# Double key loading, longer value runs and a re-planned layer norm in a fused attention and feed-forward block

## The chip, the cores and the metric

The kernel runs on one core of a Trainium2 chip. The metric is the device time of one execution in microseconds (us). A core has five engines with an instruction queue each: PE (TensorE, matrix products), DVE (VectorE), ACT (ScalarE), POOL (GpSimd) and SP (SyncE, which here issues nearly all DMAs). Each runs its own queue in order and waits on semaphores for the others. PE writes into PSUM, which has eight banks of 128 x 512 fp32; everything else lives in SBUF (128 partitions) or in device memory.

## The reference, cut to what matters

One transformer block with modulation by a condition vector c. S = 2048 positions, D = 576, H = 32 heads of 18, F = 4608, all fp32:

```python
sa, ca, ga, sb, cb, gb = six rows of (silu(c) @ w_mod)      # each of length D
h = layernorm(x) * (1 + ca) + sa
q, k, v = split(h @ wqkv)                                    # 32 heads of 18
p = softmax(q k^T * 18**-0.5)                                # 32 x 2048 x 2048
x = x + ga * ((p v) @ wo)
h = layernorm(x) * (1 + cb) + sb
out = x + gb * (silu(h @ w1) @ w2)
```

## The kernel before

**Arithmetic.** PE multiplies fp32 values in a rounded form; where that is too coarse, each operand is split into a high and a low part and three products (high-high, high-low, low-high) are added. A weight or activation therefore exists twice (`hh`/`hl`, `th`/`tl`, planes 0 and 1 of `w1t`, `w2t`, `wo`).

**Stages.** `start_tasks` (L1064) does the first layer norm, part of the q, k and v projections and the first 40 slots of scores. q and k go to device memory (`qscr`, `kscr`) in a layout that has the high and low parts of a head's 18 rows as 54 rows, v to `vscr`. Then comes attention over four blocks of 512 queries; in a block, eight quads of four heads. The output of block b is projected by `wo`, added to x, normalised again and sent through the feed-forward part while the attention of block b+1 runs. During the first block there is no feed-forward work yet, and the rest of the q and k projections fills PE instead. After the attention of the last block the feed-forward part of that block runs alone (the tail).

**Slots.** A quad of 512 queries x 2048 keys is 32 slots of two half slots. A half slot of pass a (`slot_a`, L682) multiplies 128 queries by 512 keys into a bank `psa` (`slot_mm`, L672), and DVE takes the row maximum (L680); that gives the score that softmax subtracts. 40 slots later (`LEAD`), pass b (`slot_b`, L711) computes the same scores transposed, 128 keys by 512 queries, with the maximum as two more rows of the operand, into a bank `psb`, and ACT takes the exponential into a tile `pt` (L727). The matmuls of the two passes use 64 of PE's rows each, and one of each runs at the same time. When the exponentials of a key tile (128 keys, four heads) are done, `run_pv` (L747) multiplies them by v: four heads beside each other, 32 columns of PE each, into `psv` (L762). A "value run" is the row of key tiles that are multiplied without anything between.

**Keys.** `load_k` (L645) loads 512 keys of a quad as four DMAs of 54 rows into two of 14 tiles `kts`, a ring. The same tile serves pass a and, 40 slots later, pass b. `slot_load` (L665) asks for the next keys eight slots ahead. SP issues the DMA when the tile's last reader is done.

**Order on PE.** The order of PE's instructions is written by hand, by a planner that runs while the program is built (`Plan`, L92). It keeps a time for PE and queues for ACT and DVE with fixed costs (`TS`, `TV`, `TX`, `TMAX`, `TEXP`, L73), knows when a bank comes free (`ring`, `take`, `when`), and in the main loop (L1440) chooses the next piece: a half slot, a value run of n ready key tiles, or a piece of the "filler" (q and k projections, later projection and feed-forward, L266), whose `need` says when a piece may start. `pace` spreads the filler over the slots. A value run is chosen when three key tiles are ready, when the filler has nothing ready and two are, or when there is nothing else. The other engines' instructions, the DMAs on SP among them, are ordered by the framework's own scheduler.

**Filler of a block** (`post`, L847). First `o_T` (L855) splits the attention output `ou` into `th` and `tl`; the two last row tiles wait for the time `o["at", b]` that `out_b` (L771) estimates from the last quad's DVE work. Then, for each of four row tiles, `proj` (28 pairs of half matmuls into two banks `psF`), `add_x1` and the layer norm: `ln_a` (statistics, `ln_rstd`) straight after the row tile, `ln_c` (apply) in the middle of the next. None of the layer norm's DVE work is entered in the planner's DVE queue, and `ln_at` is the plan's time plus 4500 ns. What is left of the feed-forward part of the block before (`left`) stands between the row tiles. Then the transposes `h_T`, and `mlp1`/`mlp2`. `out_b` sends the 18 rows of each head from `ov` to their place in `ou`, by SP; for the fifth row tile, of 64 rows, the rows are sent twice, to partitions 0 to 63 and 64 to 127.

**Banks.** From the first block's end on (`open_mlp`, L801) three banks are the filler's (`psF`), two row scores' (`psA`), two transposed scores' (`psB`), one the values'.

Of the kernel before, what the change touches and what calls it, by code (L numbers as in the profile page):

```python
# [18 lines left out]
P = 128  # L19
S = 2048  # L20
# [9 lines left out]
NKC = S // 512  # L30
# [13 lines left out]
NKB = 14  # L44
# [17 lines left out]
PB = 7  # L62
# [18 lines left out]
STAND = 0  # L81

# [250 lines left out]
def tile_adaln_block(ctx: ExitStack, tc: tile.TileContext, x, wqkv, wo, w1, w2, c, wfirst, wcol, out):  # L333
# [14 lines left out]
    kts = [at1.tile([P, 512], F32R, name=f"kt{i}") for i in range(NKB)]  # L348
# [26 lines left out]
    def ln_rstd(pool, mv, n):  # L375

        eng = nc.vector if pool is mp.get("p") else nc.gpsimd
        ve = pool.tile([P, n], F32, name="ve", bufs=4)
        eng.tensor_scalar_add(ve, mv[:, :, 1], EPS)
        r0 = pool.tile([P, n], F32, name="r0", bufs=4)  # L380
        nc.gpsimd.tensor_tensor(r0, ve, mhalf[:, :n], op=ALU.pow)

        t1 = pool.tile([P, n], F32, name="t1", bufs=4)
        eng.tensor_mul(t1, r0, r0)
        eng.tensor_mul(t1, t1, ve)
        eng.tensor_scalar(t1, t1, -0.5, 1.5, op0=ALU.mult, op1=ALU.add)
        rs = pool.tile([P, n], F32, name="rs", bufs=4)
        eng.tensor_mul(rs, r0, t1)
        return rs
# [196 lines left out]
    state = {"now": 0, "p": 0, "k": 0, "b": 0, "tail": False, "tail2": False}  # L586
# [42 lines left out]
    def load_quad(i):  # L629
# [13 lines left out]
        t["mx"] = at1.tile([P, 4, NST, NKC], F32, tag="mx", name="mx", bufs=2)  # L643

    def load_k(i, kc):  # L645
        qd = i % NQUAD
        for hp in range(2):
            kt_ = kts[state["k"] % NKB]
            state["k"] += 1
# [4 lines left out]
            quads.setdefault(i, {})["k", kc, hp] = kt_  # L654
# [10 lines left out]
    def slot_load(s):  # L665
# [3 lines left out]
        if (s + KLD) % 8 == 0 and 32 <= s + KLD < 32 * NQ:  # L669
            load_k(*divmod((s + KLD) // 8, 4))  # L670

    def slot_mm(s, j):  # L672
# [6 lines left out]
           rhs=t["k", kc, hp][64 * j:64 * j + 54, :], start=True, stop=True)  # L679
# [31 lines left out]
    def slot_b(s, j):  # L711
# [3 lines left out]
        if j == 0:  # L715
            if w == 0:
                t["P"] = {}
# [7 lines left out]
        mm(ps, lhsT=t["k", kt // 4, hp][64 * e:64 * e + 56, kt % 4 * P:(kt % 4 + 1) * P],  # L725
# [45 lines left out]
    def out_b(i, ov):  # L771
# [13 lines left out]
        nc.vector.transpose(ov, tt)  # L785
        chain([("V", 700), ("V", 260), ("V", 460), ("V", 700)], plan.t + 700, None, lambda at: o.update({("at", b): at + 5500}))
        for h in range(4):
            c0 = 72 * qd + DH * h
            while c0 < 72 * qd + DH * h + DH:
                kt, r0 = divmod(c0, P)  # L790
                n = min(72 * qd + DH * h + DH - c0, P - r0)
                p0 = 32 * h + c0 - 72 * qd - DH * h
                for r in (r0, r0 + 64) if kt == 4 else (r0,):
                    nc.sync.dma_start(ou[r:r + n, kt, :], ov[p0:p0 + n, :])
                c0 += n
# [5 lines left out]
    def open_mlp():  # L801
# [5 lines left out]
        psF = ctx.enter_context(tc.tile_pool(name="psF2", bufs=3, space=PSUM))  # L807
        psA = ctx.enter_context(tc.tile_pool(name="psA2", bufs=2, space=PSUM))
        mp["p"] = ctx.enter_context(tc.tile_pool(name="mlp", bufs=1, side="right"))
        plan.ring("f", 3)  # L810
        plan.ring("b", 2)
        plan.ring("a", 2)
# [34 lines left out]
    def post(b):  # L847
# [7 lines left out]
        def o_T(kt):  # L855
# [4 lines left out]
            plan.op("A", plan.t, 600)  # L860
            nc.scalar.activation(hi, src, AF.Copy)
            eng = nc.vector if last and kt % 2 == 0 else nc.gpsimd
            if kt < 4:
                eng.tensor_tensor(c["tl"][:, kt, :], src, f(hi), op=ALU.subtract)
            else:
                eng.tensor_tensor(hi[64:], src[64:], f(hi)[64:], op=ALU.subtract)
# [24 lines left out]
        def ln_a(j):  # L891
            mv = pool.tile([P, 1, 2], F32, name="mv2", bufs=4)
            ln_stats(pool, c["x1"][j], mv[:, 0, :])
            c["ln_at", j] = plan.t + 4500
            c["ln", j] = mv, ln_rstd(pool, mv, 1)

        def ln_c(j):
            mv, rs = c["ln", j]
            if j == 0:
                c["ob"] = att.tile([P, NST, 640], F32, tag="o", name="ob", bufs=1)  # L900
            ln_apply(c["x1"][j], c["ob"][:, j, :], mv[:, 0, :], rs, nc.vector)
# [655 lines left out]
```

## Time and profile before

| | |
|---|---|
| median of 3 runs | 2501.65 us (2499.65 to 2503.61) |
| profiled execution | 2500.9 us, its span 2499.1 us |
| mean granted TensorE clock | 0.984 |
| busy share of the span: PE, DVE, ACT, POOL | 96%, 72%, 60%, 25% |
| DMA | 377.78 MB, mean 151 GB/s |
| DMAs of keys (L652) | 512 of 108 KB |

How to read it: busy times are the time in which an engine had an instruction of that group under way; two matmuls at the same time count once. PEclk is the share of the full TensorE clock that was granted. A row of the view of waits has who waited, for whom, the total in us, how often, and the longest. A row of the timeline has the start in us, the length in us, the engine and line, output and inputs, how many instructions were merged, and the idle time before them with what ended it. A row of the table by stretches has, for each engine, busy us and the number of instructions, then the granted clock, the DMA share and GB/s.

### The profile page before, as it was taken

Reading aid. Unit: us, or ns where it says so; the run is one execution under the profiler, and the core shown is the slowest. Engines: PE = TensorE matmul, PEld = TensorE weight load, DVE = VectorE, ACT = ScalarE, POOL = GpSimd, SP = SyncE. Lnnn points to the kernel's source line nnn. Section 1 sums busy time; section 2 is a strip of 40 time slices with the busy share of each in tenths; the row PEclk is TensorE's granted clock in tenths of the full one; section 3 lists DMA queues with packets and bytes.
Section 4 is the critical chain, followed back from the end, with each engine's and each line's share of the span. In section 5 each row is a group of like instructions: output and inputs, shape, how many; then the busy total and the mean of one; then the engine's idle time right before and its main releaser. Section 6 shows DMA issues by size and latency. Waiting matters only on the chain.

```text
span 2499.1 us, 51105 instructions
## 1 busy us (share of the span) xinstructions
PE 2392.5 (96%) x19952; PEld 1568.9 (63%) x19952; DVE 1802.2 (72%) x3107; ACT 1495.2 (60%) x2736; POOL 633.4 (25%) x766
## 2 busy tenths in 40 slices
PE   6999999997899999998999999999999999999999
PEld 4874444434466666665666666666666666678988
DVE  7868888876788787786877777777877777324333
ACT  4237777774567666665666666665766666742121
POOL 4201111122576666653211111112211111110000
PEclk9999999998899999999999999998999999999999
DMA  7843344342465555543534333442533443226463
GB/s 241 257 137 112 113 124 124 104 149 87 134 204 178 182 188 188 179 164 127 193 129 151 128 124 129 144 141 82 204 129 130 151 146 136 96 94 236 171 224 118
DMA packets 170183, 377.78 MB, mean 151 GB/s; under 512 B 27006, under 2 KB 63262, under 8 KB 169942
## 3 DMA queue, kind: packets, MB, share of 16 engines
q1 hardware_dynamic: 165350, 372.22, 44.1%
q8 instruction: 158, 2.59, 0.4%
q10 hardware_dynamic: 4592, 2.29, 0.4%
q14 instruction: 83, 0.68, 0.1%
HBM read 282.87 MB, written 86.33 MB: 148 GB/s over the span
## 4 chain that ended last, share of the span: by engine, by line
PE 80%; DVE 9%; issue 4%; ACT 3%; DMA 2%; POOL 1%; SPq 1%; ACTq 0%; DVEq 0%; POOLq 0%
PE ps L470 25%; PE psv L762 17%; PE psa L678 13%; PE ps L464 9%; PE psb L725 8%; DVE mx L680 3%; PE psqk L551 3%; PE psv L470 2%; PE psp L470 1%; DVE etmp L988 1%; ACT pt L727 1%; DMA qt<-qscr 1%; ACT etmp L987 1%; PE psv L1213 1%; DVE hh L399 1%
## 5 line engine op out<-in xcount | busy, mean ns | idle before, releaser
L680 DVE TENSOR_REDUCE mx<-psa 128x1 f32<-128x512 f32 x2048 | 1343.7, 685 | 378.8 <-PE psb L725 269.3
L727 ACT ACTIVATE pt<-psb 128x512 f32<-128x512 f32 x2048 | 1160.0, 598 | 566.6 <-PE psb L725 413.9
L678 PE MATMUL psa<-kt,qt 54*128 54x512 f32 x2048 | 775.5, 429 | 43.6 <-DVE mx L680 39.7
L725 PE MATMUL psb<-qt,kt 56*128 56x512 f32 x2048 | 795.3, 433 | 4.4 <-ACT pt L727 2.8
L678 PEld LDWEIGHTS psa<-kt,qt 54*128 54x128 f32 x2048 | 345.3, 186 | 454.8 <-DVE mx L680 311.5
L762 PE MATMUL psv<-pt,vt 128*32 128x512 f32 x4096 | 540.9, 608 | 1.0 <-ACT pt L727 1.0
L470 PE MATMUL ps<-w2t,g 64*128 64x288 f32 x4992 | 418.6, 295 | 3.6 <-DVE x L885 3.6
L470 PEld LDWEIGHTS ps<-w2t,g 64*128 64x128 f32 x4992 | 391.3, 188 | 38.9 <-issue 10.1
L470 PE MATMUL ps<-hh,w1t 64*128 64x512 f32 x2160 | 386.6, 394 | 0.2
L725 PEld LDWEIGHTS psb<-qt,kt 56*128 56x128 f32 x2048 | 348.8, 186 | 36.1 <-ACT pt L727 24.4
L470 PEld LDWEIGHTS ps<-hh,w1t 64*128 64x128 f32 x2160 | 222.7, 186 | 54.6 <-issue 13.0
L991 POOL TENSOR_TENSOR g<-etmp,g 128x512 fp32r<-128x512 f32 x108 | 140.2, 1313 | 408.8 <-ACT g L990 408.7
L889 POOL TENSOR_TENSOR x<-x,gt 128x288 f32<-128x288 f32 x116 | 92.7, 800 | 456.2 <-ACT gt L888 456.2
L762 PEld LDWEIGHTS psv<-pt,vt 128*32 128x32 f32 x4096 | 91.2, 109 | 175.7 <-issue 165.0
L470 PE MATMUL ps<-hl,w1t 64*128 64x512 f32 x864 | 188.2, 393 | 0.0
L885 DVE TENSOR_TENSOR x<-ps,x 128x288 f32<-128x288 f32 x184 | 83.5, 454 | 119.8 <-PE ps L464 74.8
L464 PE MATMUL ps<-w2t,g 128*128 128x288 f32 x960 | 133.2, 299 | 5.1 <-ACT g L990 3.8
L464 PEld LDWEIGHTS ps<-w2t,g 128*128 128x128 f32 x960 | 130.8, 191 | 8.0 <-ACT g L990 4.3
L987 ACT ACTIVATE eq<-ps 128x512 f32<-128x512 f32 x36 | 21.5, 598 | 146.4 <-PE ps L464 146.4
L464 PE MATMUL ps<-hh,w1t 128*128 128x512 f32 x360 | 106.9, 391 | 0.5 <-DVE hh L405 0.5
L470 PEld LDWEIGHTS ps<-hl,w1t 64*128 64x128 f32 x864 | 94.3, 186 | 14.9
L988 DVE SCALAR_TENSOR_TENSOR etmp<-etmp 128x512 f32<-128x512 f32 x108 | 80.6, 777 | 17.0 <-ACT etmp L987 16.9
(139 smaller groups left out, 2035.7 us busy)
## 6 DMA issues: line engine op xcount, KB each, us to landing
w1t<-w1s SPq DMA_DIRECT2D x108, 640.0 KB
w2t<-w2s SPq DMA_DIRECT2D x108, 576.0 KB
kt<-kscr SPq DMA_DIRECT2D x512, 108.0 KB
w1s<-w1t SPq DMA_DIRECT2D x36, 640.0 KB
w2s<-w2t SPq DMA_DIRECT2D x36, 576.0 KB
vt<-vscr SPq DMA_DIRECT2D x32, 608.0 KB
qt<-qscr SPq DMA_DIRECT2D x128, 108.0 KB
raw<-in_w SPq DMA_DIRECT2D x72, 160.0 KB
```

What stands on the lines that cost most here:

```text
L464: mm(self.ps[late], lhsT=lhsT, rhs=rhs, start=(i == 0), stop=(i == self.n - 1))
L470: done = mm(self.ps[g], lhsT=lhsT[rows], rhs=rhs[rows], start=(s == 0), stop=(s == 2 * self.n - 1))
L551: mm(qk_ps[0], lhsT=w[b][:, kt, :], rhs=(hTl if a else hTh)[:, kt, n * 512:(n + 1) * 512], start=(i == 0), stop=(i == 13))
L678: mm(ps, lhsT=t["q"][64 * j:64 * j + 54, hp, stt * P:(stt + 1) * P], rhs=t["k", kc, hp][64 * j:64 * j + 54, :], start=True, stop=True)
L680: return lambda: nc.vector.tensor_reduce(t["mx"][:, 2 * j + hp, stt, kc:kc + 1], ps, axis=AX.X, op=ALU.max)
L725: mm(ps, lhsT=t["k", kt // 4, hp][64 * e:64 * e + 56, kt % 4 * P:(kt % 4 + 1) * P], rhs=t["q"][64 * e:64 * e + 56, hp, :], start=True, sto ...
L727: nc.scalar.activation(t["P"][kt, hp][:, e, :], ps, AF.Exp, scale=SCALE)
L762: mm(t["ps"][32 * h:32 * h + 32, :], lhsT=t["v"][:, c0:c0 + 32], rhs=t["P"][kt, h // 2][:, h % 2, :], start=(kt == 0), stop=(kt == NKT - 1 ...
L885: nc.vector.tensor_add(c["x1"][j][:, hs], ps, c["x1"][j][:, hs])
L889: nc.gpsimd.tensor_add(c["x1"][j][:, hs], c["x1"][j][:, hs], t)
L988: nc.vector.scalar_tensor_tensor(t, t, 1.0, u, op0=ALU.add, op1=ALU.mult)
L991: (nc.vector if last else nc.gpsimd).tensor_tensor(g[:, 1, :], t, f(g[:, 0, :]), op=ALU.subtract)
```

## The change

- **Keys** are loaded twice: pass a reads them from a ring of four tiles (`kas`), pass b loads them again into another ring of four (`kbs`). Only the first 1024 keys of the first quad are read by both from the second ring. The two rows for the maximum are set up in 4 tiles instead of 14 (8 small DMAs instead of 28).
- **Exponential tiles**: 10 instead of 7, in the space that the keys gave up.
- **Value runs**: `PVMAX` 5 instead of 3 ready key tiles end the wait at once, `PVMIN` 3 instead of 2 when the filler has nothing ready.
- **Banks** from `open_mlp` on: row scores three, filler two.
- **Layer norm** after the projection: in four steps at four places of the next row tile's projection (last row tile: with the left-over feed-forward pieces between), each entered in the planner's DVE queue.
- **Waiting for the attention output**: `o["at", b]` is unset until the plan has done the last quad's DVE work, and the projection also waits for the last `th`.
- **Output transfers**: the fifth row tile's 64 rows are sent once; the low part for partitions 64 to 127 is now made by DVE from partitions 0 to 63.

The diff, without the parts that only pass a new name on:

```diff
-NKB = 14
+NKA, NKB = 4, 4
-PB = 7
+PB = 10
+PVMAX, PVMIN = 5, 3
...
+def head_rows(h):
+    kt, r0 = divmod(DH * h, P)
+    n = min(P - r0, DH)
+    return [(kt, r0, 0, n)] + ([(kt + 1, 0, n, DH)] if n < DH else [])
...
+    def load_k(ring, n):
+        i, kc = divmod(n, NKEY)
         qd = i % NQUAD
+        tiles = kas if ring == "a" else kbs
         for hp in range(2):
-            kt_ = kts[state["k"] % NKB]
-            state["k"] += 1
+            kt_ = tiles[state["k" + ring] % len(tiles)]
+            state["k" + ring] += 1
...
         if (s + KLD) % 8 == 0 and 32 <= s + KLD < 32 * NQ:
-            load_k(*divmod((s + KLD) // 8, 4))
+            load_k("a", (s + KLD) // 8)
...
         if j == 0:
+            if s % 8 == 0 and s and s + 8 < 32 * NQ:
+                load_k("b", s // 8 + 1)
...
+        o["at", b] = None
         chain([("V", 700), ("V", 260), ("V", 460), ("V", 700)], plan.t + 700, None, lambda at: o.update({("at", b): at + 5500}))
         for h in range(4):
-            ...
-                for r in (r0, r0 + 64) if kt == 4 else (r0,):
-                    nc.sync.dma_start(ou[r:r + n, kt, :], ov[p0:p0 + n, :])
+            for kt, r0, d0, d1 in head_rows(4 * qd + h):
+                nc.sync.dma_start(ou[r0:r0 + d1 - d0, kt, :], ov[32 * h + d0:32 * h + d1, :])
...
-        psF = ctx.enter_context(tc.tile_pool(name="psF2", bufs=3, space=PSUM))
-        psA = ctx.enter_context(tc.tile_pool(name="psA2", bufs=2, space=PSUM))
+        psF = ctx.enter_context(tc.tile_pool(name="psF2", bufs=2, space=PSUM))
+        psA = ctx.enter_context(tc.tile_pool(name="psA2", bufs=3, space=PSUM))
...
+            o["th"] = None
+            chain([("A", 600)], plan.t, None, lambda at: o.update(th=at + 1500))
+            n = P if kt < 4 else 64
+            nc.scalar.activation(hi[:n], src[:n], AF.Copy)
+            eng = nc.vector if last and kt % 2 == 0 or kt == 4 else nc.gpsimd
...
+                eng.tensor_tensor(hi[64:], src[:64], f(hi)[:64], op=ALU.subtract)
...
+        def ln_steps(j):
+            return [lambda: ln_stat(j, 0), lambda: ln_stat(j, 1), lambda: ln_rs(j), lambda: ln_c(j)]
...
-            fl.add(1, lambda kt=kt: o_T(kt), need=lambda kt=kt: o["at", b] if kt > 2 else 0)
+            fl.add(1, lambda kt=kt: o_T(kt), need=(lambda: o["at", b]) if kt > 2 else None)
...
+            return None if at is None or o["th"] is None else max(at, o["th"])
...
+            steps_ = dict(zip((1, 4, 8, 11), ln_steps(j - 1))) if j else {}
...
-        if n >= 3 or n and more and not room and (ahead < 0 or not busy):
+        if n >= PVMAX or n and more and not room and (ahead < 0 or not busy):
...
-        elif n >= 2 and not busy:
+        elif n >= PVMIN and not busy:
...
-        elif n >= 2 or n and stood >= STAND:
+        elif n >= PVMIN or n and stood >= STAND:
```

93 lines of the change are left out of this document (46 added, 47 removed).

## The prediction

> **What bounds the kernel now.** I read the page first, then a table by stretches of its span, then PE's timeline where the stretches differ.
>
> ```profile
> span 2499.1 us, 51105 instructions
> PE 2392.5 (96%) x19952; PEld 1568.9 (63%) x19952; DVE 1802.2 (72%) x3107; ACT 1495.2 (60%) x2736; POOL 633.4 (25%) x766
> PE 80%; DVE 9%; issue 4%; ACT 3%; DMA 2%; POOL 1%; SPq 1%; ACTq 0%; DVEq 0%; POOLq 0%
> ```
>
> PE holds 80% of the chain that ended last. But a busy PE is not a PE at its peak, so two things decide: how much of its busy time is lost at a change from one kind of matmul to another, and where it stands or runs slowly. The table by stretches (us; busy time of PE, PEld, DVE, ACT, POOL; granted clock, DMA share, GB/s) has the cuts where the filler goes over from one block to the next:
>
> ```profile
> 575.00:600.00 25.00, 13.51 (x88) 7.56 (x90) 10.99 (x19) 9.75 (x18) 2.53 (x2) 0.76 0.36 109
> 600.00:656.00 56.00, 44.79 (x359) 25.64 (x357) 36.70 (x79) 23.74 (x43) 20.39 (x34) 0.80 0.28 94
> 656.00:1138.00 482.00, 473.53 (x4400) 308.35 (x4398) 385.61 (x614) 329.84 (x595) 299.51 (x409) 1.00 0.54 178
> 1138.00:1184.00 46.00, 38.47 (x350) 24.52 (x346) 27.55 (x50) 23.68 (x45) 13.40 (x14) 0.89 0.36 116
> 1184.00:1685.00 501.00, 496.53 (x4718) 331.36 (x4716) 396.51 (x663) 338.88 (x618) 81.67 (x81) 1.00 0.41 142
> 1685.00:1726.00 41.00, 35.34 (x316) 23.38 (x314) 26.17 (x48) 22.32 (x43) 12.96 (x13) 0.83 0.30 97
> ```
>
> In the long stretches PE is 98 to 99% busy at full clock while DVE has 80% and ACT 68%: PE bounds them, and only fewer or cheaper PE steps make them shorter. In the four short ones PE is idle for 11.5 + 11.2 + 7.5 + 5.7 = 35.9 us and the clock falls to 0.76 to 0.89.
>
> **The change, part by part.**
>
> *Value runs.* PE's timeline around one run of one key tile (x8), and runs of two (x16) and three (x24):
>
> ```profile
> 1253.86 0.39 PE L725 MATMUL psb<-qt,kt 56*128 56x512 f32 x1
> 1254.09 0.39 PE L470 MATMUL ps<-hl,w1t 64*128 64x512 f32 x2
> ...
> 1255.94 0.39 PE L678 MATMUL psa<-kt,qt 54*128 54x512 f32 x1
> 1255.96 0.39 PE L725 MATMUL psb<-qt,kt 56*128 56x512 f32 x1
> 1256.28 1.07 PE L762 MATMUL psv<-pt,vt 128*32 128x512 f32 x8
> 1257.27 0.50 PE L678 MATMUL psa<-kt,qt 54*128 54x512 f32 x1
> ...
> 1257.61 0.56 PE L470 MATMUL ps<-w2t,g 64*128 64x288 f32 x6
> ```
> ```profile
> 1217.00 1.93 PE L762 MATMUL psv<-pt,vt 128*32 128x512 f32 x16
> 1218.86 0.66 PE L910 MATMUL psT<-ident,ob 128*128 128x128 f32 x4
> ```
> ```profile
> 1462.25 2.78 PE L762 MATMUL psv<-pt,vt 128*32 128x512 f32 x24
> 1464.97 0.73 PE L470 MATMUL ps<-hh,w1t 64*128 64x512 f32 x4
> ```
>
> From the first value matmul to what follows takes 0.99, 1.86 and 2.72 us, so a key tile costs 0.865. A pair of scores holds PE for 0.23 (1253.86 to 1254.09). From the pair at 1255.94 to the end of the pair behind the run (1257.61) are 1.67 us, and the work in it is 0.23 + 0.865 + 0.23 = 1.325: a run costs 0.345 beside its work. All instructions and sizes on PE stay; the built order of the changed program has fewer runs. By block they were 128, 104, 105, 105 and are 128, 74, 73, 75: none fewer in the first block, 92 in the others. 92 x 0.345 = 32 us less. Lower bound: the 0.125 inside the run alone, 12 us; upper 32, as no row shows more per run. I take 32, because the rows before and behind the run show the rest too.
>
> The Trainium skill (TensorEngine Tiling (Array Packing), Key Properties under Tiling Modes) says that a change of the tiling mode drains TensorE, without a figure; the 0.345 is the figure here.
>
> *Going over between blocks.* What PE waits for from 580 to 690, and from 1135 to 1185 (last row), and who is behind the wait for `th`:
>
> ```profile
> PE psa L678 <- DVE mx L680: 13.7, 11, 3.3
> PE psp L470 <- ACT th L861: 9.0, 2, 4.8
> ```
> ```profile
> PE psa L678 <- DVE mx L680: 5.4, 4, 2.2
> ```
> ```profile
> 595.40 0.63 ACT L861 ACTIVATE th<-ou 128x512 fp32r<-128x512 f32 x1 [5.56 <-DMA ou<-ov]
> ```
> ```profile
> 586.89 6.81 SPq L794 DMA_DIRECT2D ou<-ov  x9
> ```
>
> The projection is begun before the attention output is in `ou`: `o["at", b]` still has the quad before's time. ACT, in order, stands on the DMA, and with it the exponentials behind it. The change unsets that time, and also waits for `th`; and the last quad sends five pieces instead of nine, 4 x 0.76 = 3 us sooner. The waits for `mx` fall where DVE does layer norm that the planner doesn't know; now it does, and a third `psA` bank gives 0.69 us of slack. What is late next is the filler itself: until `th` is there, only scores and values can run. Between the last piece of w1 and the next filler piece, the built order now has 11 half slots and 6 key tiles where 9 and 2 stood, 11 x 0.23 + 6 x 0.865 + 4 runs x 0.345 = 9.1 us of PE work: about what the wait for `ou` lasts.
>
> How much clock goes with it: the sum of the eight stretches in which half the clock was granted (588 to 1725), and two of them:
>
> ```profile
> 588.20:601.80 13.60, 6.38 (x37) 5.43 (x39) 2.04 (x3) 2.94 (x5) 2.53 (x2) 0.50 0.10 24
> 1178.70:1182.10 3.40, 3.40 (x26) 3.22 (x28) 1.86 (x3) 1.19 (x2) 0.00 (x0) 0.50 0.00 0
> sum 58.00, PE 42.97 PEld 26.06 DVE 23.90 ACT 22.04 POOL 22.01; mean PE 5.37 PEld 3.26 DVE 2.99 ACT 2.76 POOL 2.75
> ```
>
> At full clock the 43.0 busy us would be 21.5. So the bounds of this part are 0 and 35.9 + 21.5 = 57 us gained; a loss is excluded only as far as the built order holds enough work. I take 20 of the idle time and 10 of the clock, 30 us, about the middle, since the first block's passage is still paced by DVE and a stall that only shrinks can still cost clock.
>
> The Trainium skill (TensorE: Matmul & The Clock Gate, HAM oscillation) asks for no idle gap above about 3.4 us. By that all passages with shorter stalls would run at full clock and the sum would be 11 us lower. The trace differs: the half-clock stretch at 1178.70 follows waits of at most 2.2 us, so the measurement decides.
>
> *Keys twice.* 504 more DMAs of 108 KB on SP. A batch of four, and when batches come; SP's waits for a landing and for POOL; and all that PE waited for from 1185 to 1680:
>
> ```profile
> 1332.43 3.09 SPq L652 DMA_DIRECT2D kt<-kscr  x4
> ...
> 1349.09 2.37 SPq L652 DMA_DIRECT2D kt<-kscr  x4
> ```
> ```profile
> SPq L709 <- DMA mscr<-mt: 49.4, 31, 4.0
> SPq L825 <- POOL w2t L829: 42.2, 23, 8.4
> SPq L830 <- POOL w1t L829: 52.7, 29, 6.4
> ```
> ```profile
> PE psa L678 <- DVE mx L680: 2.8, 5, 0.7
> PE ps L470 <- DVE x L885: 1.1, 1, 1.1
> ```
>
> No PE wait is for a key DMA. Batches are 16.7 us apart, two now take 6.2 us of the queue and land some 1.6 (49.4 / 31) to 4 us later, so 6 us or more stay. Pass a even gains room, as its tiles come free by its own reads. In the second block, where weights are prepared by POOL, key loads stand in SP's queue behind stores that wait for POOL. I take +3 us; bounds 0, and for the late case the rival below. The Trainium skill (DMA: Bandwidth & Descriptors, Anatomy of one DMA) gives about 2.0 us as the fixed part of a DMA; bare on each of the 126 added batches, that would be an estimate of 252 us slower.
>
> *Ten exponential tiles* only let runs grow. During a run ACT has two banks to empty, 2 x 0.598 = 1.20 us (page, L727 below), DVE now three, 2.06 instead of 1.37.
>
> ```profile
> L680 DVE TENSOR_REDUCE mx<-psa 128x1 f32<-128x512 f32 x2048 | 1343.7, 685 | 378.8 <-PE psb L725 269.3
> L727 ACT ACTIVATE pt<-psb 128x512 f32<-128x512 f32 x2048 | 1160.0, 598 | 566.6 <-PE psb L725 413.9
> ```
>
> Runs of 2, 3 and 4 were 52, 9, 0 and become 83, 32, 5. ACT starves in them for 0.66, 1.52 and 2.4 us: 48 us before, 115 after, 67 more. In those stretches ACT is idle for a third of the time, so it catches up; I take +4, bounds 0 and 67. DVE starves less than before.
>
> *At no cost:* two filler banks instead of three (a next pair now needs both banks emptied, some 0.5 to 0.8 us; the scores and values between two pairs are 1.65 us of work or more in nearly all cases; bare, 174 pairs x 0.5 = 87 us); the layer norm's pieces (same DVE instructions); the shifted low part on DVE instead of POOL; 20 fewer small DMAs at the start (the first matmuls keep their order but for four transposes); the tail, whose matmul order is the same. Each is bounded by a few us either way.
>
> **Sum.** -32 - 30 + 3 + 4 = -55 us against the profiled 2500.9, which is 0.75 below the median: 2445.9, or 2446 for the median. No change means within 0.2%, 5 us, about what a measurement of this kernel can tell.
>
> **Rivals.**
> 1. *The passages keep their cost* (other waits take the stalls' place, the clock falls all the same). -32 + 7 = -25: 2476. For it: DVE paces the first passage (36.70 of 56). Against: the stall on `th` has a plain cause that goes. 0.17.
> 2. *ACT starves in the longer runs* and half of the 67 us lands on PE: 2446 - 4 + 33 = 2475; with all of it 2509. Against: 32% idle ACT. 0.11.
> 3. *Slower: key loads of pass b come late in the second block.* Two waits for POOL ahead of a batch (8.4 + 6.4 us) use up the 6 us and leave PE standing for some 7; at 16 of its 32 batches 112 us: 2558. It decides from 55 / 32 = 1.7 us a batch. For it: POOL's 299.51 of 482. Against: no wait for keys so far. 0.10.
> 4. *The passages cost nothing any more:* 27 us better than forecast: 2419. 0.12.
>
> That fewer runs are not built is excluded by the order; in the first block nothing changes.
>
> **How the numbers follow.** The forecast, 2425 to 2468 by its own terms, has 0.50. The range of 2415 to 2495 takes in rivals 1, 4 and most of 2, and leaves out rival 3, the end of 2 and what lies below, some 0.16. Faster: 0.50 + 0.17 + 0.12 + 0.08 of rival 2 = 0.87; same 0.02; slower 0.11.
>
> **What would show it.** Right: value runs at 0.345 beside their work in about 92 fewer places; the long stretches some 10 us shorter each; no wait of the projection for `th`; PEclk at 0.9 or more at the passages; no PE wait for a key DMA. Wrong: a DMA of keys among PE's releasers, with clock dips at the bounds of 512 keys; exponentials as PE's releaser behind runs of three; passages as long as before.

## The result, and the profile after

| | before | after |
|---|---|---|
| median (lowest to highest) | 2502.63 us (2499.65 to 2507.86), 4 runs | 2464.59 us (2454.58 to 2468.10), 4 runs |
| profiled execution, its span | 2500.9, 2499.1 us | 2463.14, 2461.4 us |
| mean granted TensorE clock | 0.984 | 0.981 |
| DMA | 377.78 MB | 433.01 MB |

The ratio is 0.9839, with an interval of 0.9806 to 0.9873: 38 us faster. The prediction was 2446 (2415 to 2495). On another chip the same kernel gave 2465.69 us and a ratio of 0.9856 (0.9834 to 0.9878), so the 38 us stand, and so do the 19 us by which the prediction asked for too much.

The first lines of the page of the changed kernel, with the row of DMA rates in 40 slices and the shares of the chain that ended last:

```profile
span 2461.4 us, 52349 instructions
PE 2359.8 (96%) x19952; PEld 1585.1 (64%) x19952; DVE 1789.9 (73%) x3110; ACT 1497.0 (61%) x2736; POOL 628.6 (26%) x763
...
GB/s 242 250 154 151 147 150 161 143 160 146 144 202 195 227 227 209 206 211 164 182 147 202 171 178 157 164 179 117 217 176 162 155 197 165 133 90 241 183 214 119
...
PE 82%; DMA 6%; DVE 5%; POOL 2%; ACT 2%; issue 2%; SPq 1%; ACTq 0%; POOLq 0%; DVEq 0%
```

PE has the same 19952 instructions. DVE's share of the chain fell from 9% to 5%, and DMA's rose from 2% to 6%: what PE waits for has changed. The table by stretches (us; busy time of PE, PEld, DVE, ACT, POOL; granted clock, DMA share, GB/s) shows where. The cuts lie at about the same places of the work as in the prediction, so the later stretches are shorter:

```profile
575.00:600.00 25.00, 17.09 (x88) 6.27 (x80) 15.53 (x27) 12.79 (x24) 1.27 (x1) 0.83 0.45 145
600.00:656.00 56.00, 51.06 (x404) 29.46 (x400) 39.65 (x89) 26.67 (x48) 23.60 (x37) 0.84 0.39 131
656.00:1138.00 482.00, 466.11 (x4394) 323.06 (x4396) 377.70 (x608) 326.87 (x593) 295.57 (x407) 0.98 0.63 203
1138.00:1184.00 46.00, 41.11 (x394) 25.86 (x392) 31.34 (x57) 26.65 (x51) 12.28 (x12) 0.93 0.45 148
1184.00:1660.00 476.00, 473.20 (x4637) 327.02 (x4636) 389.51 (x659) 338.25 (x613) 81.15 (x81) 1.00 0.53 174
1660.00:1700.00 40.00, 33.72 (x302) 20.59 (x300) 25.32 (x39) 22.08 (x42) 9.87 (x8) 0.91 0.41 137
```

The long stretch of the second block (656 to 1138) had PE busy for 473.53 us at full clock before; now it is busy for 466.11 at 0.98, and DMA moves 203 GB/s where it moved 178. In the third block (1184 to 1660) PE misses only 2.8 of 476 us, and 4.5 of 501 before. All that PE waited for in the second block's long stretch:

```profile
PE psb L739 <- DMA qt<-mscr: 7.8, 3, 3.4
PE psb L739 <- ACT pt L741: 5.3, 5, 1.7
PE psb L739 <- DMA kb<-kscr: 1.9, 3, 0.8
PE psa L690 <- DVE mx L692: 0.6, 1, 0.6
```

Before, they were these two, and none was for a transfer:

```profile
PE psa L678 <- DVE mx L680: 5.7, 11, 1.2
PE ps L470 <- DVE x L885: 1.4, 2, 1.1
```

`qt<-mscr` are the row maxima of a quad on their way through device memory into the rows of pass b's operand.

**The account.** To compare equal work, both traces are cut where the same matmuls end: the last value run of the quad before a block's last one, and the last of the transposes that end the passage into the next block's feed-forward part. "Work" is the sum over the matmuls in a piece at the rates of undisturbed rows (a pair of scores 0.231 us, a key tile 0.858, and so on); "rest" is wall time less work less 0.345 us per value run.

| piece | wall us, before / after | value runs | rest us | change of rest |
|---|---|---|---|---|
| first block | 360.6 / 360.4 | 112 / 112 | 44.4 / 44.2 | -0.2 |
| passage 1 | 134.5 / 130.9 | 27 / 29 | 57.0 / 51.5 | -5.5 |
| second block, long stretch | 420.7 / 417.7 | 84 / 54 | 20.0 / 34.5 | +14.5 |
| passage 2 | 137.4 / 140.9 | 24 / 23 | 18.8 / 14.0 | -4.8 |
| third block, long stretch | 406.7 / 378.9 | 82 / 51 | 12.2 / 7.1 | -5.1 |
| passage 3 | 135.5 / 145.8 | 24 / 23 | 16.9 / 15.4 | -1.5 |
| fourth block, long stretch | 404.5 / 373.9 | 81 / 53 | 13.9 / 7.4 | -6.5 |
| last quad and passage to the tail | 95.8 / 109.0 | 13 / 10 | 13.5 / 16.3 | +2.8 |

Some feed-forward work has moved over the cuts, which wall time shows and "rest" does not. The sum: 92 runs fewer x 0.345 = -31.7, the rest -6.3, together -38.0 us, which is the difference of the last matmuls' ends (2495.6 and 2457.6). So the value runs give nearly all, the passages 11.8, the third and fourth block 11.6, and the second block's long stretch takes 14.5 back. The 0.345 is the prediction's price, not one measured anew over whole pieces: were it higher, part of what the rest of the third and fourth block lost would be the runs' too.

### The profile page after: what moved, and what is told of

It is laid out like the page before. It is cut to its first block, busy times and chain, and to the rows that moved or that the text cites. A ratio compares the mean times of both kernels' runs of the same rounds, so it can differ in the third digit from the quotient of the medians.

```text
span 2461.4 us, 52349 instructions
## 1 busy us (share of the span) xinstructions
PE 2359.8 (96%) x19952; PEld 1585.1 (64%) x19952; DVE 1789.9 (73%) x3110; ACT 1497.0 (61%) x2736; POOL 628.6 (26%) x763
## 2 busy tenths in 40 slices
DMA packets 201458, 433.01 MB, mean 176 GB/s; under 512 B 31354, under 2 KB 67610, under 8 KB 201210
## 4 chain that ended last, share of the span: by engine, by line
PE 82%; DMA 6%; DVE 5%; POOL 2%; ACT 2%; issue 2%; SPq 1%; ACTq 0%; POOLq 0%; DVEq 0%
PE ps L480 25%; PE psv L776 17%; PE psa L690 12%; PE ps L474 10%; PE psb L739 8%; PE psqk L561 4%; DVE mx L692 2%; PE psv L480 2%; PE psp L480 1%; DMA raw<-in_w 1%; DMA mscr<-mt 1%; PE psv L1238 1%; PE psqk L1238 1%; PE psqk L480 1%; PE psp L474 1%
## 5 line engine op out<-in xcount | busy, mean ns | idle before, releaser
L739 PE MATMUL psb<-qt,kb 56*128 56x512 f32 x2048 | 772.6, 427 | 39.2 <-ACT pt L741 22.0
L690 PE MATMUL psa<-ka,qt 54*128 54x512 f32 x2016 | 739.4, 420 | 10.9 <-DVE mx L692 8.7
L690 PEld LDWEIGHTS psa<-ka,qt 54*128 54x128 f32 x2016 | 344.1, 188 | 316.3 <-DVE mx L692 213.4
L776 PE MATMUL psv<-pt,vt 128*32 128x512 f32 x4096 | 521.4, 608 | 2.0 <-ACT ov L780 2.0
L739 PEld LDWEIGHTS psb<-qt,kb 56*128 56x128 f32 x2048 | 357.4, 187 | 90.3 <-ACT pt L741 61.0
L480 PEld LDWEIGHTS ps<-hh,w1t 64*128 64x128 f32 x2160 | 216.4, 186 | 60.6 <-DVE mx L692 10.9
L776 PEld LDWEIGHTS psv<-pt,vt 128*32 128x32 f32 x4096 | 98.5, 109 | 211.7 <-issue 203.4
L480 PE MATMUL ps<-hl,w1t 64*128 64x512 f32 x864 | 181.1, 392 | 0.0
```

The lines of the kernel that those rows point to most:

```text
L480: done = mm(self.ps[g], lhsT=lhsT[rows], rhs=rhs[rows], start=(s == 0), stop=(s == 2 * self.n - 1))
L690: mm(ps, lhsT=t["q"][64 * j:64 * j + 54, hp, stt * P:(stt + 1) * P], rhs=t["a" if ("a", kc, hp) in t else "b", kc, hp][64 * j:64 * j + 54, ...
L739: mm(ps, lhsT=t["b", kt // 4, hp][64 * e:64 * e + 56, kt % 4 * P:(kt % 4 + 1) * P], rhs=t["q"][64 * e:64 * e + 56, hp, :], start=True, sto ...
L776: mm(t["ps"][32 * h:32 * h + 32, :], lhsT=t["v"][:, c0:c0 + 32], rhs=t["P"][kt, h // 2][:, h % 2, :], start=(kt == 0), stop=(kt == NKT - 1 ...
```

## The experiments

Three questions: what the second loading of the keys costs and by what (its places in SP's queue behind waits for POOL, or its bytes), what the passages still wait for, and what the value runs, the banks and the planned layer norm are worth one by one. Medians are compared with the changed kernel's 2464.59 and 2465.69; the kernel before had medians of 2501.27 to 2504.24 on the chips used, so differences over chips of less than some 3 us mean nothing.

**1. No second loading.** Pass b's tiles are taken from the ring as they are (and the exponential's scale is cut):

```diff
...
-                load_k("b", s // 8 + 1)
+                keep_k(s // 8 + 1)
...
-        nc.scalar.activation(t["P"][kt, hp][:, e, :], ps, AF.Exp, scale=SCALE)
+        nc.scalar.activation(t["P"][kt, hp][:, e, :], ps, AF.Exp, scale=0.02 * SCALE)
```

> The changed kernel without pass b's reloads: after the first 1024 keys of the first quad its ring is not written again, so 504 DMAs of 108 KB go and the order on PE stays. It leaves out part of the computation (pass b works on old keys, and its exponentials take a fiftieth of the scale so that they stay finite). Theory A (the second loading is not hidden in the second block: the maxima's store and loads stand behind eight key DMAs in SP's queue, and PE waits 3.4 + 1.5 + 3.0 us for them and then runs at half clock): 12 to 18 us faster than the changed kernel, 2447 to 2453, with no PE wait for the maxima from 660 to 1140 and full clock there. Theory B (the loads are hidden, and the second block was no faster for another reason): within 5 us of 2465.

Measured: 2431.08 us (2423.59 to 2433.93), ratio 0.9702 (0.9660 to 0.9745), 33.5 us less than the changed kernel; the expected size was too small. By the pieces of the account, wall time falls by 8.7 in passage 1, by 15.4 in the second block's long stretch and by 3.1 in passage 2; in the third block it is 378.6 for 378.9 and in the fourth 373.7 for 373.9. The loads cost much in one block and nothing in the next two, with the same number of loads in each. These two blocks also work on old keys, so the altered values by themselves change nothing there. Theory A's sign held in part only: from 656 to 1138 PE still waits for the maxima for 4.1 us in three waits, and 3.4 us of the second block's long stretch still run at half clock. (The two profiled executions differ by 29.2 us; these three pieces make 27.2.)

**2 and 8. Taking waits out of SP's queue.** In one run POOL issues the transfers of the maxima, in another the stores of the prepared weights that wait for POOL:

```diff
-        nc.sync.dma_start(scr, t["mt"])
+        nc.gpsimd.dma_start(scr, t["mt"])
...
-            nc.sync.dma_start(f(dst), src)
+            nc.gpsimd.dma_start(f(dst), src)
```

> The changed kernel with the three DMAs of a quad's maxima issued by POOL instead of SP. Theory A (it is the place in SP's queue that makes them late): 8 to 15 us faster than the changed kernel, about 2453, the waits for them gone in the second block. Theory A2 (it is the traffic of the key loads that makes them land late): no gain, the waits stay. Theory C (POOL, busy for 62% of the second block, issues them still later): 5 to 20 us slower, with waits for the maxima at most quads of that block.

Measured: 2479.21 us (2474.38 to 2481.15), ratio 0.9901 (0.9866 to 0.9936), 15 us slower than the changed kernel.

```diff
-        nc.sync.dma_start(f(scr), f(w))
+        nc.gpsimd.dma_start(f(scr), f(w))
```

> The changed kernel with the 77 stores of prepared weights issued by POOL, which prepares them, instead of SP; the order on PE is the same. Theory A (the 24 us that the second loading of keys costs around the second block are key and maxima DMAs behind stores and loads that wait for POOL in SP's queue): SP waits some 68 us less for POOL there, 10 to 20 us faster than the changed kernel, 2445 to 2455. Theory A2 (it is the traffic, not the queue): within 5 us of 2465. Theory C (issuing takes POOL 0.6 us each, 46 us of a busy POOL, and weights come late): 5 to 15 us slower, with PE waits for w1t or w2t.

Measured: 2472.08 us (2469.26 to 2477.83), ratio 0.9880 (0.9855 to 0.9904), 7 us slower. Both times lie in the range of theory C, by which POOL issues later than SP, but its signs are missing: PE does not wait for `w1t` or `w2t` with the stores on POOL, and with the maxima on POOL its long waits come at three of the block's quads and not at most of them. In both the second block's long stretch is the longer one, 434 us by the account's cuts (417.7 in the changed kernel, 424.3 in its repeat). PE's largest wait in the second block's long stretch with the maxima on POOL:

```profile
PE psb L739 <- issue: 21.7, 3, 7.5
```

Three waits of up to 7.5 us of pass b, where the changed kernel had three of up to 3.4 for `qt<-mscr`, and up to 5.3 (14.1 us in all) in its repeat; the profile shows no releaser for them, so that these are the maxima is argued from the line and the count. With the stores on POOL, PE waits for the maxima for 13.5 us, no more than in the repeat. Freeing SP's queue of waits in this way did not pay; why it costs was not separated, and it left open whether the place in the queue or the bytes are the price.

**10. The loads in their places, without their bytes.** Each second load brings 6 rows of 54; number and places of the DMAs stay. The rest of those tiles keeps old keys, and the exponential's scale is cut as in 1. The kernel repeated beside it gave 2465.69 us.

```diff
...
+                rows = 2 if ring == "b" and n > 1 else DH
+                nc.sync.dma_start(f(kt_[64 * j:64 * j + 3 * rows, :]),
...
```

> The changed kernel with each of pass b's reloads cut from 54 rows to 6; the DMAs, their places in SP's queue, their waits and the order on PE stay, a ninth of the bytes moves. It leaves out part of the computation (pass b has old keys in 48 of 54 rows, and its exponentials take a fiftieth of the scale so that they stay finite). Theory Q (the second loading costs its 24 to 30 us around the second block by its places in SP's queue): within 6 us of the changed kernel. Theory T (by its bytes, which make the other transfers land later): 18 to 30 us faster than it, like the kernel without reloads.

Measured: 2438.90 us (2434.55 to 2442.03), ratio 0.9753 (0.9731 to 0.9776): 27 us less than the repeat, of the 33 that leaving the loads out gave. What costs is mostly the bytes. PE's two largest waits in the second block's long stretch, and that stretch in the table:

```profile
PE psb L740 <- ACT pt L742: 5.3, 4, 2.0
PE psb L740 <- DMA qt<-mscr: 3.5, 3, 1.9
```
```profile
656.00:1138.00 482.00, 471.01 (x4488) 323.39 (x4484) 390.09 (x626) 337.73 (x614) 303.04 (x411) 0.99 0.58 187
```

The page gives these loads 12 KB each and the kernel 383.46 MB. The rate falls from 203 to 187 GB/s, the wait for the maxima from 7.8 to 3.5 us. The account's piece is 400.7 us instead of 417.7: PE stands for 7.5 us instead of 15.9, and 0 us instead of 17.1 run at half clock. At half the rate 17.1 us lose 8.5, an estimate, so the two make 16.9 of the 17.0. Against the repeat, whose piece is 424.3 us with 21.6 us of standing and 23.9 at half clock, the same sum gives 26 for 23.6, so it is good to some us and no better.

How the wait for the maxima becomes lost time is best seen where it is longest. SP's queue in the changed kernel, and PE behind it:

```profile
725.44 1.22 SPq L664 DMA_DIRECT2D ka<-kscr  x2
726.71 0.73 SPq L664 DMA_DIRECT2D kb<-kscr  x2
...
729.05 0.35 SPq L717 DMA_DIRECT2D mscr<-mt  x1
733.72 1.37 SPq L721 DMA_DIRECT2D qt<-mscr  x2
```
```profile
732.72 0.39 PE L739 MATMUL psb<-qt,kb 56*128 56x512 f32 x1
...
736.75 0.47 PE L739 MATMUL psb<-qt,kb 56*128 56x512 f32 x1 [3.41 <-DMA qt<-mscr]
737.15 2.49 PE L776 MATMUL psv<-pt,vt 128*32 128x512 f32 x16
```
```profile
738.40:741.80 3.40, 3.40 (x18) 1.81 (x12) 1.29 (x2) 1.08 (x2) 0.00 (x0) 0.50 0.70 224
```

Eight key loads are issued, then the maxima go out; it takes 729.05 + 0.35 to 733.72, 4.3 us, until they have landed and may come back. PE stands for 3.41 us, and 1.6 us after it goes on, the clock is at half for 3.4 us.

The bytes alone do not make this wait. The kernel with the old banks (6) loads the keys twice too, and DMA moves 206 GB/s in this stretch, but PE waits for the maxima for only 1.8 us there (and once for 1.8 us with no releaser shown):

```profile
PE psb L739 <- DMA qt<-mscr: 1.8, 2, 0.9
```

The kernels without a second load still wait for them, 4.1 us (1) and 4.9 us (11); the kernel before did not. So the rest of the change, the new order on PE above all, has a part in the wait, and how the two divide it was not separated.

**3 and 4. The high part of the attention output on POOL.** The last two `th` of a block are made by POOL instead of ACT, so that ACT does not stand on `ou<-ov`; in the second run the maxima are issued by POOL too.

```diff
...
+            if kt > 2 and not last:
+                o["th"] = plan.t + 2700
+                nc.gpsimd.tensor_copy(hi[:n], src[:n])
...
```

> The changed kernel with the last two high parts of the attention output copied by POOL instead of ACT in all blocks but the last; the order on PE is nearly the same. Theory A (ACT, in order, stands on the landing of the attention output with exponentials behind it, and that is why the passages between blocks keep most of their cost): PE's waits of 5.0, 2.9 and 2.9 us near 592, 1150 and 1673 go, and half of the 17 us of half clock behind them: 12 to 20 us faster than the changed kernel, 2445 to 2453. Theory B (the projection waits as long for POOL's copy, so the stall only moves): within 5 us of 2465, with PE waits for th or tl in place of those for pt.

Measured: 2454.58 us (2453.77 to 2459.99), ratio 0.9811 (0.9776 to 0.9845), 10 us less than the changed kernel: 5.0 in passage 2 and 5.7 in passage 3, nothing in passage 1. ACT in passage 2 of the changed kernel, and PE behind it:

```profile
1147.69 0.60 ACT L741 ACTIVATE pt<-psb 128x512 f32<-128x512 f32 x1 [0.21 <-PE psb L739]
1151.77 0.63 ACT L872 ACTIVATE th<-ou 128x512 fp32r<-128x512 f32 x1 [3.47 <-DMA ou<-ov]
1152.30 1.06 ACT L741 ACTIVATE pt<-psb 128x512 f32<-128x512 f32 x2
```
```profile
1149.52 0.50 PE L690 MATMUL psa<-ka,qt 54*128 54x512 f32 x1
1152.93 1.28 PE L739 MATMUL psb<-qt,kb 56*128 56x512 f32 x2 [2.91 <-ACT pt L741]
```

With POOL taking that step, POOL is what waits, until 1153.94, and ACT's exponentials go on in the meantime:

```profile
1149.22 0.60 ACT L741 ACTIVATE pt<-psb 128x512 f32<-128x512 f32 x1 [0.21 <-PE psb L739]
1150.64 2.28 ACT L741 ACTIVATE pt<-psb 128x512 f32<-128x512 f32 x4 [0.82 <-PE psb L739]
```
```profile
1153.94 0.61 POOL L872 CAST th<-ou 128x512 fp32r<-128x512 f32 x1 [4.81 <-PE psb L739]
```

Passage 1 shows why nothing came there. The stall went to the next engine that waits in order: DVE, which the change gave the fifth row tile's low part, stands on POOL's `th`, the row maxima stand behind it, and PE waits for them:

```profile
601.49 0.69 DVE L881 TENSOR_TENSOR th<-ou,th 64x512 fp32r<-64x512 f32 x1 [5.28 <-POOL th L872]
```
```profile
602.95 0.79 PE L690 MATMUL psa<-ka,qt 54*128 54x512 f32 x1 [5.34 <-DVE mx L692]
```

Over the span PE's wait for exponentials falls from 22.0 to 11.8 us, and its wait for `mx` rises from 8.7 to 16.2. Theory A holds in passages 2 and 3, theory B, with another wait than it named, in passage 1.

> The changes of the two kernels before this one together; the order on PE is that of the kernel with the copies on POOL. If both theories A hold and the causes are separate, the gains add: 2430 to 2442. If POOL becomes the bound of the second block, it is slower than the kernel with the copies alone.

Measured: 2464.00 us (2458.90 to 2466.79), ratio 0.9841 (0.9806 to 0.9877). The gain of the one and the loss of the other nearly cancel: the second block's long stretch is 435 us, as in 2, and passage 2 is as short as in 3. The expected 2430 to 2442 rested on a gain in 2 that was not there.

**5. Short runs again.** All of the change but the run rule:

```diff
-PVMAX, PVMIN = 5, 3
+PVMAX, PVMIN = 3, 2
```

> The changed kernel with the old rule for value runs (three ready key tiles end the wait, two when the filler has nothing). The built order has 92, 88 and 91 runs in the blocks after the first in place of 74, 73 and 75: 49 more. Theory A (each run costs 0.345 us beside its work, whatever else): 17 us slower than the changed kernel, 2482. Theory B (longer runs starve ACT and give part of it back): less than 8 us slower, with fewer PE waits for pt.

Measured: 2504.12 us (2500.26 to 2515.25, 10 runs), ratio 1.0011 (0.9995 to 1.0028): the rest of the change, together, gives nothing that can be measured, although it already has 43 of the 92 fewer runs, and the run rule on top of it gives about 39 us. By the account's pieces there are 49 more value runs than in the changed kernel, and 49 x 0.345 = 17, so neither theory has the size. The profile is of the slowest of the ten executions, 52 us longer than the changed kernel's, and it can be taken apart: 17 us for the runs, 17 us in which PE stands longer (its total wait for exponentials is 39.1 us, 22.0 in the changed kernel), 24 us more at half clock, which lose some 12 (the first passage has 50.9 for 37.5), and about 6 left over. Why the short runs bring these waits was not separated.

**6. The old banks.** Three filler banks, two for row scores, everything else as changed:

```diff
-        psF = ctx.enter_context(tc.tile_pool(name="psF2", bufs=2, space=PSUM))
-        psA = ctx.enter_context(tc.tile_pool(name="psA2", bufs=3, space=PSUM))
+        psF = ctx.enter_context(tc.tile_pool(name="psF2", bufs=3, space=PSUM))
+        psA = ctx.enter_context(tc.tile_pool(name="psA2", bufs=2, space=PSUM))
...
```

> The changed kernel with the old split of banks from the first block's end on: two for row scores, three for the filler. The built order then has 98, 100 and 94 value runs, 70 more than the changed kernel: the planner no longer lets the runs grow. Theory A (the third bank is what lets runs be long, and it takes waits for mx out besides): 70 x 0.345 = 24 us for the runs and 8 to 14 us in the long stretches, 2497 to 2503, no faster than the kernel before. Theory B (the bank matters by the order alone): 2489. Theory C (it is worth nothing): 2465.

Measured: 2479.43 us (2478.23 to 2483.98), ratio 0.9909 (0.9888 to 0.9931), 15 us slower, between theories C and B; the 24 us of theory A for the runs alone are not reached. The third bank is no free edit: without it the built order has 70 more value runs, and the long stretches of the third and fourth block are 15 and 18 us longer. But passage 1 is 12 us shorter (118.7 for 130.9), so there the three filler banks did better in this profile.

**7. The old planning.** The four steps of the layer norm, their entries in the planner's DVE queue and both waits for the attention output are undone (the shorter transfers stay):

```diff
-        o["at", b] = None
...
-            o["th"] = None
-            chain([("A", 600)], plan.t, None, lambda at: o.update(th=at + 1500))
+            plan.op("A", plan.t, 600)
...
-            return None if at is None or o["th"] is None else max(at, o["th"])
+            return None if at is None else max(at, o["at", b])
...
-        for step in ln_steps(3):
-            if b == 0:
-                fl.add(700)
-            rest(2)
-            fl.add(0, step)
+        if b == 0:
+            fl.add(3000)
+        rest(6)
+        fl.add(0, lambda: ln_c(3))
...
```

> The changed kernel with the layer norm in two steps that the planner does not enter, and with the old times for the attention output; fewer transfers, banks and runs stay. The built order has 210 runs against 222, worth 4 us. Theory A (planning is worth 15 us or more in the passages): 2476 or slower. Theory B (the passages are set by ACT's wait for the attention output, which planning does not move): 2460 to 2470.

Measured: 2450.23 us (2447.99 to 2457.98), ratio 0.9786 (0.9763 to 0.9810): 14 us faster than with the planning, of which the 12 fewer runs are worth 4. Neither theory has it: both expected 2460 or more. The passages are 3.5, 3.9 and 3.7 us shorter. The profiled execution, at 2457.98, is the slowest of its runs, and in it the second block's long stretch is 9 us longer, so it shows less of the gain than the median. What PE waits for here, from its list for the whole span:

```profile
PE psa L690 <- DVE mx L692: 8.8, 17, 1.7
...
PE psp L480 <- ACT th L870: 4.5, 1, 4.5
```

The wait of the projection for `th` is back, 4.5 us, and the kernel is faster all the same; the waits for `mx` are as in the changed kernel (8.7), so it was not the planned layer norm that removed them.

**11. One ring again, long runs kept.** The 14 key tiles, one loading and 7 exponential tiles of before, with the new run rule, banks and planning:

```diff
-NKA, NKB = 4, 4
+NKA, NKB = 14, 14
-PB = 10
+PB = 7
...
+    kbs = kas
...
-                load_k("b", s // 8 + 1)
...
```

> The changed kernel with the keys loaded once into a ring of 14 tiles and 7 exponential tiles, as before the change; banks, the rule for value runs, layer norm and transfers stay changed. The built order has 244 value runs after the first block against 222. Theory A (double loading and ten tiles buy 22 runs, 8 us, and cost the 24 to 33 us that the kernel without reloads gained): 16 to 25 us faster than the changed kernel, 2440 to 2449. Theory B (the exponential tiles are what lets ACT run on through the value runs, as the short runs' 40 us suggest): no faster than the changed kernel, with PE waits for pt in the long stretches.

Measured: 2463.32 us (2461.06 to 2467.17), ratio 0.9852 (0.9831 to 0.9874), no different from the repeat. Beside the repeat, passage 1 is 4.3 and the second block's long stretch 11.9 us shorter (5.3 beside the first profile), and the long stretches of the third and fourth block are 7.3 and 11.7 longer, with 9 and 5 value runs more. The time is theory B's, but its sign is not there: in the third and fourth block with passage 3 between them PE waits for `pt` for 4.8 us, no more than in the changed kernel (5.9). The double loading with ten tiles pays itself back in the later blocks, and no more.

**12. What the runs point to.** One ring, the old planning, and the last two `th` on POOL: the edits of 11, 7 and 3.

> The kernel with one ring of keys, with the layer norm and the attention output planned as before the change, and the last two high parts of the attention output copied by POOL instead of ACT. The built order has 238 value runs after the first block. If the three gains are separate (16 to 25 us of the ring, 10 of the copies, 5 to 14 of the old planning): 2420 to 2435. If the passages cannot gain twice: 2435 to 2445.

Measured: 2434.30 us (2430.10 to 2439.17), ratio 0.9735 (0.9713 to 0.9758), 31 us less than the changed kernel on the same chip and 68 less than the kernel before. One by one the three edits gave 2, 14 and 10 us, some 5 less than together; the ring's 16 to 25 did not come by itself. From its table by stretches:

```profile
600.00:656.00 56.00, 52.87 (x466) 32.12 (x466) 50.92 (x106) 37.56 (x67) 27.62 (x42) 1.00 0.38 121
656.00:1138.00 482.00, 474.46 (x4584) 325.02 (x4578) 389.56 (x630) 333.95 (x610) 304.09 (x413) 1.00 0.57 186
1138.00:1184.00 46.00, 43.30 (x438) 28.95 (x434) 41.03 (x91) 29.65 (x54) 13.35 (x17) 1.00 0.54 184
```

These three stretches had clocks of 0.84, 0.98 and 0.93 in the changed kernel. Passage 1 is not free of half clock: 20.5 us of it lie before 600, where the changed kernel has 37.5 in the whole passage.

## Why the prediction was right or wrong

**Direction and range held**; the time was 19 us too low. The likeliest case was given 2425 to 2468, and the result lies at its upper end. That it lies inside is in part luck: the passages fell short by 18 us and the second block's long stretch lost 11.5 more than forecast, and a gain in the third and fourth block, which no term had, made good 12 of it. Three terms failed: the passages, the second loading and the banks. A fourth, the value runs, held by itself but has an effect beside it that the sum did not have.

*Value runs, -32: held in number and place.* 92 fewer, none in the first block. Runs of one, two and three tiles take 0.996, 1.855 and 2.713 us in the median, as before, and of four 3.571, so nothing was paid inside them. But the run rule alone, undone, costs 39 us, not 17: besides its own 0.345 a run has an effect on the waits and the clock that the sum did not have.

*Passages, -30: wrong by 18.* The three passages gave 5.5 + 4.8 + 1.5 = 11.8 us. The forecast said that the stall on `th` has a plain cause that goes. The wait did go from the projection, but the cause, ACT standing in order on `ou<-ov` with exponentials behind, stayed: PE's wait `psb <- pt` rose from 2.8 to 22.0 us over the span. Without the planning it is 21.1, so it was not the planning that brought it; with the step on POOL it is 11.8. The prediction had named "the exponentials behind it" and then priced only the projection. Experiment 3 shows 10 us of it by another engine alone, and in passage 1 the same thing again one engine further. Rival 1, that other waits take the stalls' place, is nearer to this term than the forecast. The planning itself, which was to give the gain, costs 14 us, 4 of them by 12 more runs; why the other 10 was not separated. Without it the rest of the passages falls by 22.0 us against the kernel before instead of 11.8, so what they gained came from the other edits.

*Keys twice, +3: wrong in size, and the rival had the mechanism wrong.* Leaving out the loads gives 33 us, leaving out their bytes 27; the bare estimate of 252 us is far off. The forecast looked for a PE wait on a key DMA and found in it the test: that wait is 1.9 us in the second block's long stretch. The transfer that came late was another one, the maxima, which cross device memory twice in sequence (SP's wait for the first landing, then the second), and in this profile each of these waits that was longer than 1 us had a stretch of half clock behind it. Rival 3 had the right block and the right side, but put the price on the places behind POOL's waits in SP's queue and on key loads; taking waits off that queue (2 and 8) made it worse, and thinning the bytes helped. Which transfers delay which, byte by byte, was not settled, nor how much of the wait comes from the rest of the change (experiment 10). One row speaks against a simple story: SP's mean wait for the maxima's landing in this stretch is 14.1 / 8 = 1.8 us before and 20.3 / 7 = 2.9 after, but it is 17.2 / 6 = 2.9 in the last experiment too, where PE waits for the maxima for 1.3 us only.

*ACT starvation, +4 (0 to 67): the low end.* PE's wait for exponentials from 1184 to 2096, the third and fourth block with passage 3, which has the longest of them:

```profile
PE psb L739 <- ACT pt L741: 5.9, 6, 2.9
```

That is 5.9 us in 912, for runs of up to four tiles, of which passage 3 has 5.2; with the 5.3 of the second block's long stretch some 6 us lie outside the passages, close to the +4. The rest of the third and fourth block fell. Rival 2 is out.

*At no cost: one of them was a gain.* Two filler banks and three for row scores were taken as nothing; undoing them costs 15 us net, more than that in the later blocks and less than nothing in passage 1. The rest of the third and fourth block fell by 5.1 + 6.5 us, which the forecast did not have; undoing the banks, and going back to one ring with seven tiles, each lose it.

In sum, against -32 - 30 + 3 + 4 = -55: runs -31.7, passages -11.8, second block's long stretch +14.5, third and fourth block -11.6, the end +2.8, start and first block -0.2: -38.

*What would show it:* the long stretches lost 28 to 31 runs each, worth some 10 us, as said, but the second block's is only 3.0 us shorter in all; no wait of the projection for `th`, as said; PEclk at 0.9 or more held at the second and third passage (0.93, 0.91) and not at the first (0.83, 0.84); no PE wait for a key DMA failed by 1.9 us for `kb` in the second block, and by one of 5.0 us put down to `ka` in the first passage. That last one is the second row here:

```profile
596.32 0.63 ACT L872 ACTIVATE th<-ou 128x512 fp32r<-128x512 f32 x1 [5.65 <-DMA ou<-ov]
...
597.49 1.28 PE L739 MATMUL psb<-qt,kb 56*128 56x512 f32 x2 [5.03 <-DMA ka<-kscr]
```
```profile
597.49 0.28 PEld L739 LDWEIGHTS psb<-qt,kb 56*128 56x128 f32 x1 [5.34 <-ACT pt L741]
```

The matmul reads `qt` and `kb`, not `ka`; ACT had stood on `ou<-ov` until 1.2 us earlier with exponentials behind, and the load of the same matmul's weights, the last row, is put down to `pt`. So this too was the exponentials, and not a key DMA.

## What to carry to other kernels

Where an in-order engine waits for a transfer, letting the consumer of its result wait can change the place of the stall and not the stall: ask what else stands in that engine's queue, give the step to an engine that has nothing urgent behind it, and then ask the same of whoever reads its result. Bytes that PE hardly waits for can still have a price: price them in the stretch where small dependent transfers are due, by leaving the bytes out there, and not by the mean. A change of many parts that wins as a whole can hold parts that lose; undoing two of them and moving one step to another engine found 31 us here.

## What the runs showed of the hardware that was not expected

A wait of PE of 1.46 us was followed by half clock. The two waits and the stretches behind them, from the changed kernel's second block:

```profile
789.39 0.66 PE L739 MATMUL psb<-qt,kb 56*128 56x512 f32 x1 [1.71 <-ACT pt L741]
...
999.87 0.72 PE L739 MATMUL psb<-qt,kb 56*128 56x512 f32 x2 [1.46 <-DMA qt<-mscr]
```
```profile
789.60:793.00 3.40, 3.40 (x24) 3.28 (x25) 1.80 (x6) 1.81 (x4) 0.00 (x0) 0.50 0.77 206
1001.20:1004.60 3.40, 3.40 (x28) 3.22 (x26) 1.67 (x4) 1.70 (x4) 2.34 (x4) 0.50 0.67 211
```

Of the gaps in PE's work longer than 1 us from 545 to 2190 in this trace, all of 1.36 us and more had a half-clock stretch running or beginning within 1.7 us of their end, but for one of 1.55 us at 2176; the three of 1.02 to 1.14 had none. All 14 traces together give no sharp bound: a half-clock stretch went with 54 of 54 gaps of 3 us and more, with 47 of 70 from 1.4 to 3 us, and with 8 of 61 from 1 to 1.4. In experiment 3 a wait of 2.95 us for the maxima was followed by full clock:

```profile
1072.90 0.47 PE L739 MATMUL psb<-qt,kb 56*128 56x512 f32 x1 [2.95 <-DMA qt<-mscr]
```

By the Trainium skill (TensorE: Matmul & The Clock Gate, HAM oscillation) the rule is no idle gaps above about 3.4 us. The measurement decides: much shorter ones can cost clock here, and their length alone does not say which. The granted clock was 1.0 or 0.5 and nothing between in all 14 traces, and the half-clock stretches inside them lasted 3.41 us or a multiple of it, up to 5. What else the clock looks at was not tried.

The 33 us of the second loading appear at 203 GB/s, while the page shows slices of 242 and 250 GB/s at the start: so this price was paid below the highest rate seen.

One stretch varies and the others do not: the repeat has the third block's long stretch at 378.9 us and the fourth's at 374.0, within 0.1 of the first profile, but the second block's at 424.3 instead of 417.7. PE's wait for the maxima in it is 14.1 us in the repeat and 7.8 in the first profile, so single profiles of that stretch are good to some 7 us.
